# Delta-rule attention in units of 64 tokens of all batches, with the inverse turned on VectorE

## The chip, the core and the metric

The kernel runs on one core of one Trainium2 chip. Its time is the device time of one execution in microseconds (us). A core has TensorE (PE in the profile, its weight loads PEld), VectorE (DVE), ScalarE (ACT), GpSimd (POOL) and SyncE (SP), which here issues every DMA. Each engine works through its own instructions in order and waits for others by semaphores.

## What is computed

```python
k_n = k / (np.linalg.norm(k, axis=-1, keepdims=True) + 1e-06)
state = np.zeros((B, H, D, D), dtype=np.float32)
for t in range(S):
    kt, vt, bt = (k_n[:, :, t], v[:, :, t], beta[:, :, t, None])
    y[:, :, t] = np.einsum('bhd,bhde->bhe', q[:, :, t], state)
    v_old = np.einsum('bhde,bhd->bhe', state, kt)
    state = state + bt[:, :, :, None] * np.einsum('bhd,bhe->bhde', kt, vt - v_old)
...
h = np.maximum(x @ w_in, 0.0)
return (h * h @ w_out).astype(np.float32)
```

B = 4 batches, H = 8 heads, S = 768 tokens, D = 48. `x` is `y` with the heads of a token side by side: 3072 tokens of 384, then an MLP with 2048 hidden units. All in float32.

## The kernel before

**Attention in chunks.** The recurrence is done in chunks of C = 64 tokens. Inside a chunk the tokens depend on each other through a unit lower triangular 64x64 matrix, whose inverse is called T. T is put together from 32x32 blocks (HB = 32): the diagonal blocks are inverted step by step on DVE (`invert`, L383 and L384, 31 steps), and the block below the diagonal comes from two rounds of small matmuls (`whole`, L422 and L430). A unit is 128 tokens (NC = 2 chunks) of two batches; there are 12 units. Partitions 0 to 63 hold one batch of the pair, 64 to 127 the other.

**The steps of a unit.** `load`, `load_q`, `load_v`, `load_beta` fetch rows by DMA. `normalize` (L241 to L254) divides the keys by their norms on ACT and DVE. `static` turns keys and queries by 128x128 transposes on PE (L285), multiplies them (L295), masks (L304), and sends the key products through DRAM (`blocks`, L312, L320) so that each partition of `lt` holds one 32x32 block. `invert` inverts, multiplies by beta (L386), and sends the result through DRAM again (`inv`, L390, L399, L404) into `tt` and `t1t`, which DVE turns (L415). `whole` makes the block below, and multiplies T with the keys (L442) and the values (L449). `sequential` goes through the two chunks: state products (L472), the new state (L485, L488), the output `y` (L493).

**MoE.** `moe` takes the 256 tokens of a unit: it splits `x` into a high and a low half of full speed type (fp32r), so that each product is three matmuls; L541 is the first layer, L528 the second, L548 to L551 and L520 stand between on ACT and DVE.

**The weights.** The 28 weight parts (512 or 384 columns, numbered 0 to 27 here) are split the same way, in the opening of the kernel: `least` is an ACT abs (L142) and a POOL maximum (L143), `words` four DVE operations (L150 to L157) and an ACT copy (L160), `low` three matmuls (L166) and an ACT copy (L167). `far` says how many parts `least` runs ahead: 3 below part AHEAD - 3, 1 from there on. AHEAD is 20.

**What sets the order.** PE, DVE, ACT and SP run in the order in which the program issues (`manual_schedule`); POOL's order is set by the scheduler. `weave` mixes the parts of a unit's attention, at given fractions of the unit, into MoE of the unit before as the filler. In unit 1 the remaining weight splits are mixed in too.

Of the kernel before, what the change touches and what calls it, by code (L numbers as in the profile page):

```python
# [20 lines left out]
def kernel(  # L21
# [14 lines left out]

# [37 lines left out]

    plus, minus = [const.tile([P, P], F32R, name=n) for n in ("plus", "minus")]
# [18 lines left out]
    nc.gpsimd.memset(qp[:, :, :, D:], 0.0)

    ttile = []
    for i in range(2):
        tt = const.tile([P, NC, H, C], F32, name=f"tt{i}")
        nc.gpsimd.memset(tt[:, :, :, :HB], 0.0)
        ttile.append(tt)  # L100
    state = []
    for i in range(NU):
        s = const.tile([P, 2, NP, D], F32, name=f"state{i}")
        nc.gpsimd.memset(s, 0.0)
        state.append(s)

# [13 lines left out]
    AHEAD = 20  # L120
# [67 lines left out]
    def split_bank():  # L188

        turn[1] += 1  # L190
        return (ps_o.tile([P, PC], F32, name=f"o{turn[1] % 2}") if split_early else ps_x.tile([P, PC], F32, name="x"))


    def tokens(x, d):

        t0, b0 = d["t0"], d["b0"]
        return [x[b0 + b, :, t0:t0 + P, :].rearrange("h (c t) d -> t c h d", c=NC) for b in range(2)]

    def load_to(dst, x, d, width):
        for b, src in enumerate(tokens(x, d)):  # L200
            for c in range(NC):
                nc.sync.dma_start(out=dst[b * C:(b + 1) * C, c, :, :width], in_=src[:, c])  # L202

    def load(u):
        t0, b0 = (u // NU) * P, (u % NU) * 2
        d = dict(u=u, t0=t0, b0=b0, y=[None] * NC, marks={})
        d["kp"] = kpad[u % 3]
        load_to(d["kp"], k, d, D)
        return d

    def load_q(d):

        d["qp"] = kpad[2] if d["u"] == 1 else qp
        load_to(d["qp"], q, d, D)

    def load_beta(d):

        first = d["u"] <= 1
        d["bt"] = ds_[0]["bt"] if d["u"] == 1 else apool.tile([P, HB], F32, name="bt", bufs=2)
        t0, b0, x = d["t0"], d["b0"], C * (d["u"] == 1)  # L220

        by = beta[b0:b0 + 2, :, t0:t0 + P].rearrange("b h (c n s) -> b n c h s", n=2, s=HB)
        for n in range(4):
            nc.sync.dma_start(out=d["bt"][x + n * H2:x + (n + 1) * H2], in_=by[n // 2, n % 2])
        if not first:
            nc.sync.dma_start(out=d["bt"][C:], in_=d["bt"][:C])

    def load_v(d):
        d["vt"] = apool.tile([P, NC, H, D], F32, name="vt", bufs=2)
        load_to(d["vt"], v, d, D)  # L230

    def normalize(d):

        n2, s0, s1 = [apool.tile([P, H2], F32, name=f"{n}{d['u'] % 2}", bufs=1) for n in ("n2", "s0", "s1")]
        kn = d["kp"].rearrange("p c h d -> p (c h) d")[:, :, :D]
        for c in range(NC):
            h = slice(c * H, (c + 1) * H)

            sq = (apool.tile([P, H, D], F32, name="r", bufs=2) if d["u"] == 2 else
                  spool.tile([P, PC], F32, name="rest")[:, :H * D].rearrange("p (h e) -> p h e", h=H))  # L240
            nc.scalar.activation(out=sq, in_=kn[:, h], func=AF.Square)  # L241
            nc.vector.tensor_reduce(out=n2[:, h], in_=sq, axis=AX.X, op=ALU.add)  # L242
            yield
# [3 lines left out]
        nc.vector.reciprocal(out=s1, in_=s1)  # L247
        yield
        nc.vector.tensor_tensor(out=s1, in0=s1, in1=n2, op=ALU.mult)
        nc.vector.tensor_tensor(out=s1, in0=s1, in1=s0, op=ALU.add)  # L250
        nc.vector.tensor_scalar(out=s1, in0=s1, scalar1=0.5, scalar2=1e-6, op0=ALU.mult, op1=ALU.add)
        nc.vector.reciprocal(out=s1, in_=s1)
        yield
        nc.vector.tensor_tensor(out=kn, in0=kn, in1=s1.unsqueeze(2).broadcast_to(list(kn.shape)), op=ALU.mult)  # L254
        yield

    def x_tile(u=2):

        turn[0] += 1
        pool, name = (ps_h, "h") if u <= 1 and turn[0] % 4 >= 2 else (ps_x, "x")  # L260
        return pool.tile([P, PC], F32, name=name)


    def static(d):

# [460 lines left out]
```

## Time and profile before

| | us |
|---|---|
| median of 3 runs | 705.74 |
| range of the runs | 704.6 to 705.8 |
| span of the profiled execution | 699.1 |
| PE busy in it | 635.6 (91%) |
| PEld busy | 590.5 (84%) |
| DVE busy | 429.0 (61%) |
| ACT busy | 331.7 (47%) |
| POOL busy | 69.6 (10%) |

The span goes from the first to the last instruction of the profiled execution; the times of the runs hold what lies around it as well, so their median is 6.6 us above the span. The busy shares are means over stages with different limits, and matmuls are pipelined: a busy PE isn't a PE at its peak. The views below are the table of busy times by stretch, the chain of work that ended last (followed back from the last instruction), the timeline, and the groups of like instructions.

### The profile page before, as it was taken

The numbers are of one execution on the slowest core, as the hardware profiler recorded it, in microseconds if no ns is written. First come the engines' busy times: TensorE is split into PE (matmuls) and PEld (weight loads), VectorE is DVE, ScalarE is ACT, GpSimd is POOL, SyncE is SP. The second block draws the span as 40 slices with busy tenths as digits, with TensorE's granted clock in tenths as the row PEclk, the third lists the DMA queues.
The fourth block names the chain that finished last, engine by engine and source line by source line (L and its number), as shares of the span: only waits on it lengthen the run. The fifth ranks groups of instructions, "written<-read, shape, count | busy, mean of one in ns | idle before, by whom it ended". The sixth has DMA issues, their size and how long they took to land.

```text
span 699.1 us, 23322 instructions
## 1 busy us (share of the span) xinstructions
PE 635.6 (91%) x10104; PEld 590.5 (84%) x10104; DVE 429.0 (61%) x1165; ACT 331.7 (47%) x632; POOL 69.6 (10%) x86
## 2 busy tenths in 40 slices
PE   2831789789999999999999999999999999999997
PEld 1610458679999999999999999999999999999996
DVE  4799965677477477486494683775774764731221
ACT  3730665644544544535535535545345355355352
POOL 6540422210101001001001001001010010000000
PEclk9965999999999999999999999999999999999999
DMA  7898504100531522613504405315216124030100
GB/s 160 175 303 312 89 7 80 37 2 12 110 59 24 114 42 38 123 20 54 124 3 80 99 2 112 67 17 116 48 24 123 33 41 91 3 61 3 25 1 23
DMA packets 172134, 49.92 MB, mean 71 GB/s; under 512 B 163840, under 2 KB 166912, under 8 KB 172032
## 3 DMA queue, kind: packets, MB, share of 16 engines
q1 hardware_dynamic: 172032, 48.44, 32.6%
q8 instruction: 79, 1.29, 0.8%
q14 instruction: 23, 0.19, 0.1%
HBM read 37.32 MB, written 11.01 MB: 69 GB/s over the span
## 4 chain that ended last, share of the span: by engine, by line
PE 80%; DVE 9%; SPq 3%; ACT 3%; issue 2%; DMA 1%; POOL 1%; DVEq 0%; POOLq 0%
PE h L541 29%; PE o L528 29%; PE g L472 3%; PE g L493 3%; PE g L449 3%; DVE h_h L381 2%; SPq L202 2%; DVE tt L384 2%; PE x L442 2%; PE x L485 2%; PE x L295 1%; PE g L295 1%; PE g L285 1%; PE x L285 1%; DVE a L153 1%
## 5 line engine op out<-in xcount | busy, mean ns | idle before, releaser
L528 PE MATMUL o<-w,h_h 128*128 128x384 f32 x768 | 203.4, 346 | 0.0
L541 PE MATMUL h<-x_h,w 128*128 128x256 f32 x1152 | 172.3, 285 | 2.2 <-ACT x_h L510 1.3
L520 DVE TENSOR_TENSOR h_l<-r,h_h 128x512 fp32r<-128x512 f32 x96 | 66.4, 691 | 153.0 <-PE o L528 61.7
L541 PEld LDWEIGHTS h<-x_h,w 128*128 128x128 f32 x1152 | 152.6, 188 | 6.1 <-ACT x_h L510 2.7
L548 ACT ACTIVATE r<-h 128x512 f32<-128x512 f32 x96 | 57.4, 598 | 175.1 <-PE h L541 174.8
L528 PEld LDWEIGHTS o<-w,h_h 128*128 128x128 f32 x768 | 133.1, 188 | 2.4
L528 PE MATMUL o<-w,h_l 128*128 128x384 f32 x384 | 129.8, 338 | 0.0
L383 DVE SCALAR_TENSOR_TENSOR tmp<-lt,bt,z 128x126 f32<-128x126 f32 (+22 forms) x310 | 95.8, 309 | 17.6 <-DMA lt<-blocks 8.1
L541 PE MATMUL h<-x_l,w 128*128 128x256 f32 x576 | 99.0, 280 | 0.0
L384 DVE TENSOR_TENSOR z<-z,tmp 128x126 f32<-128x126 f32 (+22 forms) x310 | 79.2, 255 | 10.7
L541 PEld LDWEIGHTS h<-x_l,w 128*128 128x128 f32 x576 | 81.4, 188 | 0.0
L528 PEld LDWEIGHTS o<-w,h_l 128*128 128x128 f32 x384 | 72.1, 188 | 0.0
L549 ACT ACTIVATE r<-r 128x512 f32<-128x512 f32 x96 | 60.7, 632 | 3.1
L551 ACT CAST h_h<-r 128x512 fp32r<-128x512 f32 x96 | 59.5, 620 | 3.1
L367 POOL MEMSET z<- 128x512 f32 x10 | 5.2, 524 | 401.0 <-DMA inv<-z 401.0
L242 DVE TENSOR_REDUCE n<-rest 128x8 f32<-128x384 f32 x22 | 12.0, 550 | 36.7 <-ACT rest L241 36.7
L143 POOL TENSOR_SCALAR a<-a 128x384 f32<-128x384 f32 (+1 forms) x18 | 24.8, 1377 | 55.7 <-ACT a L142 47.1
L166 PE MATMUL o<-r,plus 128*128 128x512 f32 (+1 forms) x16 | 8.8, 637 | 23.0 <-DVE r L153 23.0
L434 ACT ACTIVATE tt<-x 32x256 f32<-32x256 f32 x42 | 15.7, 374 | 26.6 <-PE x L430 26.1
L510 ACT CAST x_h<-h 128x384 fp32r<-128x384 f32 x24 | 11.4, 480 | 31.1 <-PE h L508 31.1
L472 PEld LDWEIGHTS g<-state,kq 48*64 48x64 f32 x1408 | 22.5, 134 | 4.3 <-issue 2.8
L472 PE MATMUL g<-state,kq 48*64 48x48 f32 x1408 | 25.3, 220 | 0.0
(141 smaller groups left out, 783.6 us busy)
## 6 DMA issues: line engine op xcount, KB each, us to landing
w<-in_moe_w_in_dram SPq DMA_DIRECT2D x12, 512.0 KB
w<-in_moe_w_out_dram SPq DMA_DIRECT2D x16, 384.0 KB
lt<-blocks SPq DMA_DIRECT2D x22, 256.0 KB
kpad<-in_k_dram SPq DMA_DIRECT2D x48, 96.0 KB
vt<-in_v_dram SPq DMA_DIRECT2D x48, 96.0 KB
out_dram<-a SPq DMA_DIRECT2D x48, 96.0 KB
qpad<-in_q_dram SPq DMA_DIRECT2D x44, 96.0 KB
blocks<-ap SPq DMA_DIRECT2D x48, 64.0 KB
```

The lines of the kernel that those rows point to most:

```text
L143: nc.gpsimd.tensor_scalar(out=a.bitcast(F32), in0=a.bitcast(F32), scalar1=LEAST, scalar2=None, op0=ALU.max)
L383: nc.vector.scalar_tensor_tensor(out=tmp, scalar=bt[:, s:s + 1], op0=ALU.mult, op1=ALU.mult, **factors)
L384: nc.vector.tensor_tensor(out=z[:, :nj, s + 1:], in0=z[:, :nj, s + 1:], in1=tmp, op=ALU.subtract)
L449: nc.tensor.matmul(g[rows, c, h], lhsT=tt[rows, c, h], rhs=vt[rows, c, h], start=True, stop=True)
L472: nc.tensor.matmul(dst[b * C:(b + 1) * C, j, p], lhsT=kq[rows, c, p, b, x], rhs=s[rows, b, p], start=(x == 0 and p == 0), stop=False, skip ...
L493: nc.tensor.matmul(gy[rows, j, p], lhsT=ap[rows, c, h, 1], rhs=uu[rows, h], start=first and p == 0, stop=True, skip_group_check=True)
L520: nc.vector.tensor_tensor(out=h_l, in0=r, in1=h_h.bitcast(F32), op=ALU.subtract)
L528: nc.tensor.matmul(o[i], lhsT=a[:, e, i * P:(i + 1) * P], rhs=halves["wo", ft][w], start=(ft == 0 and n == 0), stop=(ft == FT - 1 and n == 2))
L541: nc.tensor.matmul(hp[:, e], lhsT=halves["wi", (kt, ft // EACH)][w][:, f], rhs=x[:, kt], start=(n == 0), stop=(n == 3 * KT - 1))
L548: nc.scalar.activation(out=r, in_=hp, func=AF.Relu)
L549: nc.scalar.activation(out=r, in_=r, func=AF.Square)
L551: nc.scalar.copy(out=h_h, in_=r)
```

## The change

A unit is now one chunk of 64 tokens of all four batches (still 12 units). Even and odd heads (j = 0, 1) and batches (b) are laid out so that a head's operands can lie in the other half of the partitions than its result.

- **Raw keys.** Keys aren't normalized. Key products are made of raw keys (`key_products`), 32x32 blocks for two units (a pair) at once; the squared norms are their diagonals, and `prepare` folds the norms into beta and keeps `nr` to scale V (`scale_v`).
- **Turns on DVE.** `load_blocks` loads 32x32 blocks of keys and queries so that one DVE transpose (`turned`) gives the d-by-token form; only the first units use PE (`turned_by_pe`). The trips through DRAM go: DVE turns the key products from PSUM into `lt`, and the inverse into `zt` and `t1` (`ended`).
- **Inverse.** `invert` now always handles full 32-column blocks, for a pair of units at a time: 21 steps in the odd unit (F1 = 21), ten in the next.
- **T inside the chain.** T isn't multiplied with keys and values ahead of time (L442 and L449 go); `state_part` takes V minus the state product, multiplies by T to `w` (L402), then makes state (L412) and output (L418).
- **Splits.** AHEAD is 10. `half_of` draws further splits when MoE needs a half that isn't there.
- PSUM: one pool `g` of two double banks instead of `g` and `x`.

```diff
-    AHEAD = 20
+    AHEAD = 10
...
+    def half_of(key):
+        while key not in halves:
+            next(splits)
+        return halves[key]
...
+    def load_beta(d):
+        d["bt"] = bt = apool.tile([P, HB], F32, name="bt", bufs=1)
...
+        for b in range(2):
+            for s in range(2):
+                for j in range(2):
+                    for i in range(2):
...
+                        nc.sync.dma_start(out=bt[r0:r0 + X],
...
+    def turned(src, dst):
+        nc.vector.transpose(out=dst.rearrange("p n t -> p (n t)"), in_=src.rearrange("p n t -> p (n t)"))
...
+    def key_products(d):
+        d["diag"], low = g_tile(), g_tile()[:, 0]
+        for i in range(2):
+            kt = kts[2 * d["pair"] + i]
+            for x in range(X):
...
+                            half = kt[dims(j), b * X + x, s * HB:(s + 1) * HB]
+                            nc.tensor.matmul(d["diag"][(up, lo)[s](b), j, at], lhsT=half, rhs=half, start=True, stop=True)
...
+                        nc.tensor.matmul(low[(lo, up)[j](b), at], lhsT=first, rhs=second, start=True, stop=True)
...
+        nc.vector.transpose(out=lt.rearrange("p a b -> p (a b)"),
+                            in_=d["diag"].rearrange("p j (c t) -> p t (j c)", t=HB))
...
+    def ended(d):
+        z = d["z"]
+        nc.vector.tensor_tensor(out=z, in0=z, in1=d["bt"].unsqueeze(1).broadcast_to([P, HB, HB]), op=ALU.mult)
...
+        nc.vector.transpose(out=zt.rearrange("p j i x t -> p t (j i x)"), in_=z.rearrange("p s t -> p t s"))
+        yield
+        nc.vector.transpose(out=t1.rearrange("p j i x s -> p s (j i x)"), in_=z.rearrange("p s t -> p (s t)"))
...
-                    nc.tensor.matmul(ps[b][j * C:(j + 1) * C, c, p], lhsT=kp[rows, c, h], rhs=tt[rows, c, h],
-                                     start=True, stop=True)
...
-                    nc.tensor.matmul(g[rows, c, h], lhsT=tt[rows, c, h], rhs=vt[rows, c, h], start=True, stop=True)
...
+                    nc.tensor.matmul(ps[half_rows(b ^ j), j, x], lhsT=tt[half_rows(b), j, x], rhs=vt[half_rows(b), j, x],
+                                     start=True, stop=True)
...
-                    nc.tensor.matmul(gy[rows, j, p], lhsT=ap[rows, c, h, 1], rhs=uu[rows, h],
...
+                    nc.tensor.matmul(gy[half_rows(b), j, x], lhsT=ap[0][half_rows(b ^ j), j, x], rhs=w[half_rows(b ^ j), j, x],
...
+        take(inverse)
+        take(ended(pairs[0]))
         take(splits, 1)
...
+            if u == 1:
+                parts.append((splits, spread(0, 0.88, NW - 6), False))
...
+            if u % 2:
+                parts.append((s, [0.1, 0.5, 0.72], False))
...
+            else:
+                parts.append((inverse, spread(0, 0.26, HB - 1 - F1), True))
+                parts.append((ended(pair), [0.28, 0.30, 0.32], True))
+                parts.append((s, [0.12, 0.56, 0.76], False))
+                parts.append((query_products(u), [0.3], False))
+                parts.append((below(pair, 0), [0.38, 0.45], False))
```

The order moves at three places.

On DVE, in the opening before the first inversion: before, the four operations of a weight part (here part 6) stand ahead of the first inversion (L374 scales `lt` by beta, L381 and L384 are the steps).

```order
L153 SCALAR_TENSOR_TENSOR r<-w_153,r 128x384
L156 TENSOR_SCALAR w_153<-r 128x384
L157 SCALAR_TENSOR_TENSOR h_l<-w_153 128x384
L150 TENSOR_SCALAR a<-a 128x384
L153 SCALAR_TENSOR_TENSOR a<-w_319,a 128x384
L156 TENSOR_SCALAR w_319<-a 128x384
L157 SCALAR_TENSOR_TENSOR rest<-w_319 128x384
L374 TENSOR_TENSOR lt<-lt,bt 128x1024
L381 TENSOR_TENSOR h_h<-lt,tt_110 128x31
```

After the change, on DVE at the same place, the first part (w_130 is part 0) follows the whole inversion and the turns of its result.

```order
L312 TENSOR_TENSOR tmp<-lt,z 128x31
L314 TENSOR_TENSOR z<-z,tmp 128x31
L319 TENSOR_TENSOR z<-z,bt 128x1024
L322 STREAM_TRANSPOSE zt<-z 128x32x32
L324 STREAM_TRANSPOSE t_607<-z 128x32x32
L133 TENSOR_SCALAR a<-a 128x512
L136 SCALAR_TENSOR_TENSOR a<-w_130,a 128x512
L139 TENSOR_SCALAR w_130<-a 128x512
L140 SCALAR_TENSOR_TENSOR rest<-w_130 128x512
```

So parts 0 to 6 have moved from ahead of the first inversion to behind it.

On ACT, among the splits of parts 6 and 7 before: L160 copies the high half of part 6 and of part 7 (w_542, w_708), L167 the low half of the part before, and L142 is the abs of part 9 and of part 10 (w_333, w_335), three ahead.

```order
L160 CAST w_542<-a 128x384
L167 CAST w_505<-o_544 128x384
L142 ACTIVATE r<-w_333 128x512
L241 ACTIVATE r<-kpad_104 128x384 x2
L244 ACTIVATE s_695<-n_694 128x16
L160 CAST w_708<-r 128x512
L167 CAST w_542<-o_710 128x384
L142 ACTIVATE a<-w_335 128x384
```

After, on ACT in unit 1, where L143 copies the high half of parts 11, 12 and 13 (w_1376, w_1398, w_1431), L150 the low half of the part before each, L125 is the abs of parts 12, 13 and 14 (w_494, w_496, w_498), and L288 the square root of the norms.

```order
L143 CAST w_1376<-a 128x384
L150 CAST w_1142<-g 128x384
L125 ACTIVATE a<-w_494 128x384
L143 CAST w_1398<-a 128x384
L150 CAST w_1376<-g 128x384
L125 ACTIVATE a<-w_496 128x384
L288 ACTIVATE s_1415<-lt 128x32
L143 CAST w_1431<-a 128x384
L150 CAST w_1398<-g 128x384
L125 ACTIVATE a<-w_498 128x512
```

The abs now runs one part ahead, from part 7 on instead of from part 17 on, and stands behind the copies of the part before it.

On DVE, in an even unit (unit 2) just ahead of `below`: L246 turns the keys of the unit after next, L319, L322 and L324 are `ended`, L361 masks the query products, L443 is MoE's `h_l`.

```order
L246 STREAM_TRANSPOSE kt<-kb_82 128x1024
L312 TENSOR_TENSOR tmp<-lt,z 128x60
L314 TENSOR_TENSOR z<-z,tmp 128x30x2
L443 TENSOR_TENSOR h_l<-r,h_h 128x512
L312 TENSOR_TENSOR tmp<-lt,z 128x31
L314 TENSOR_TENSOR z<-z,tmp 128x31
L319 TENSOR_TENSOR z<-z,bt 128x1024
L443 TENSOR_TENSOR h_l<-r,h_h 128x512
L361 TENSOR_TENSOR ap<-g,mask 128x512 x2
L322 STREAM_TRANSPOSE zt<-z 128x32x32
L324 STREAM_TRANSPOSE t_2339<-z 128x32x32
L443 TENSOR_TENSOR h_l<-r,h_h 128x512 x2
```

Before, the inversion's steps ran on into the unit and its result left DVE by DMA, with one turn of 256 elements (L415) per unit; now the end of the inversion and the turns stand together in one unit of two.

More of the change, by code (lines that the diff above doesn't have):

```diff
@@ L190, in split_bank @@
         turn[1] += 1
[L191 to L202, printed above, removed]
@@ L228, in load_v @@
[L228 to L243, printed above, removed]
+        return (ps_o.tile([P, PC], F32, name=f"o{turn[1] % 2}") if split_early else g_tile()[:, 0])
@@ L435, in whole @@
         yield
[L436 to L439 removed]
+        if not last:
+            ps = wide(g_tile())
+            for x in range(X):
                 for b in range(2):
[L441 to L443 removed]
@@ L501, in moe @@
-    def moe(d):
+                    for j in range(2):
+                        nc.tensor.matmul(ps[half_rows(j), b, x], lhsT=kp[half_rows(b ^ j), j, x], rhs=w[half_rows(b ^ j), j, x],
+                                         start=True, stop=True)
+            nc.vector.tensor_tensor(out=s, in0=s, in1=ps, op=ALU.add)
+        for x in range(X):
+            for b in range(2):
+                for j in range(2):
+                    nc.tensor.matmul(gy[half_rows(b), j, x], lhsT=ap[0][half_rows(b ^ j), j, x], rhs=w[half_rows(b ^ j), j, x],
+                                     start=first and x == 0, stop=True, skip_group_check=True)
@@ L600, in loads, with weave @@
-    def loads(u):
-        if u + 2 < units:
-            ds_.append(load(u + 2))
-        if u + 1 < units:
-            load_v(ds_[u + 1])
-        yield
-        if u + 2 < units:
-            load_q(ds_[u + 2])
-            load_beta(ds_[u + 2])
-        yield
-        if u + 2 < units:
-            yield from normalize(ds_[u + 2])
-    def state_part(d):
-        yield from whole(d)
-        yield from sequential(d)
-    F0, F1, F2 = 3, 3, 6
-    NS = NW + 1 - (1 + 6 + 4 + 7)
+    def weave(filler, parts):
+        order = [(at, 0, n, gen, quiet) for gen, ats, quiet in parts for n, at in enumerate(ats)]
+        gen, n, a, b = filler
+        order += [(a + (b - a) * (m + 0.5) / n, 1, m, gen, None) for m in range(n)]
+        order = [x[3:] for x in sorted(order, key=lambda x: x[:3])]
+        apart = True
+        while order:
+            gen, quiet = order.pop(0)
+            if quiet is False and not apart and (filler[0], None) in order:
+                order.remove((filler[0], None))
+                next(filler[0], None)
+            next(gen, None)
+            if quiet is not True:
+                apart = quiet is None
@@ L651 @@
         take(splits, 1)
-        for d in pair:
-            take(d, 2)
+        for _ in below(pairs[0], 0):
             take(splits, 1)
-            take(d, 1)
+        for _ in state_part(0):
             take(splits, 1)
-            take(d, 1)
-            take(splits, 1)
-        ds_.append(load(2))
-        fetch(NW)
-        take(invert(ds_[0]))
-        load_v(ds_[1])
-        load_q(ds_[2])
-        load_beta(ds_[2])
-        third = normalize(ds_[2])
-        take(third, 3)
-        for _ in range(3):
-            take(splits, 1)
-            take(third, 1)
```

558 lines of the change are left out of this document (255 added, 303 removed).

## The prediction

> **What bounds the kernel now.** I read the page's head first, then the busy times of stretches, cut at the places where the limit changes.
>
> ```profile
> span 699.1 us, 23322 instructions
> ```
> ```profile
> 0.00:38.60 38.60, 20.81 (x310) 15.37 (x310) 24.87 (x48) 20.12 (x46) 21.05 (x33) 1.00 0.79 170
> 38.60:65.70 27.10, 2.93 (x6) 1.64 (x6) 24.94 (x65) 5.52 (x13) 7.08 (x7) 0.53 1.01 351
> 65.70:104.30 38.60, 29.64 (x514) 18.82 (x514) 31.31 (x64) 23.94 (x51) 13.61 (x11) 0.93 0.31 57
> 104.30:164.90 60.60, 54.00 (x769) 46.93 (x769) 41.66 (x106) 31.98 (x64) 10.28 (x8) 1.00 0.18 35
> 164.90:653.70 488.80, 488.80 (x8238) 468.85 (x8237) 298.53 (x873) 233.00 (x430) 17.59 (x27) 1.00 0.31 59
> 653.70:699.10 45.40, 39.43 (x270) 38.87 (x270) 7.68 (x12) 17.10 (x29) 0.00 (x0) 1.00 0.08 18
> ```
>
> Columns: stretch, length, busy time of PE, PEld, DVE, ACT, POOL, granted clock, DMA share, GB/s. From 164.9 to 653.7 (units 2 to 11) PE is busy without a gap: there a matmul saved is time saved. From 653.7 the last MoE runs alone, and nothing in it changes. Before 164.9 PE isn't the bound: from 38.6 to 65.7 it stands still while DVE inverts T for units 0 and 1, and until 164.9 the splitting of the 28 weight parts sets the pace. So two sums are made, the **opening** and the **ten PE-bound units**.
>
> **The ten units.** The chain that ended last, in one unit (start, us, line, records; each f32 matmul of the program is two records):
>
> ```profile
> 351.42 0.61 PE x L485 x32
> 352.03 0.93 PE g L493 x32
> ...
> 356.35 1.08 PE g L472 x64
> ...
> 364.67 0.33 PE h L508 x3
> ...
> 366.39 0.87 PE x L285 x8
> 367.26 0.87 PE g L285 x8
> 368.14 1.06 PE h L541 x9
> ...
> 372.37 1.03 PE x L295 x32
> 373.40 0.87 PE g L295 x32
> ...
> 381.87 0.68 PE x L422 x50
> ...
> 385.94 0.68 PE x L430 x50
> 386.62 1.25 PE h L541 x9
> ...
> 390.00 1.09 PE x L442 x64
> 391.09 1.85 PE g L449 x64
> ```
>
> L485, L493 and L472 come twice in a unit. Attention thus costs PE 1.22 + 1.86 + 2.16 + 1.74 (L285) + 1.90 (L295) + 0.68 + 0.68 + 1.09 + 1.85 = 13.2 us, 26.4 in two units. MoE's own matmuls stay. L472 and L442, which use all four 64x64 corners of the array, take 1.08 and 1.09 us for 32 matmuls: 34 ns each. L449 and L493, whose operand and result stand in the same half of the partitions (two corners on the diagonal), take 1.85/32 and 0.93/16: 58 ns.
>
> After the change, per unit, L387, L396, L402, L412, L418 and L357 are 32 matmuls each, all with four corners: 6 x 32 x 34 ns = 6.5 us. The transposes L285 and the products L442 go. Per pair of units come 128 matmuls in `below` (32x32, L422's 0.68 us for 32, 21 ns: 2.7 us) and 192 key products L266/L270. These, 48 rows by 32 columns, the trace doesn't show: 21 ns by L422 to 34 ns by L442, 4.1 to 6.5 us; I take 4.1, since the columns match L422's. Two units: 13.0 + 2.7 + 4.1 = 19.8 instead of 26.4, 6.6 less. The first group of MoE behind a piece of attention takes 0.19 longer (L541 x9: 1.25 against 1.06); the pieces fall from 16 to 13 a pair: 0.6 less. Five pairs: 36 us (what the last units lack is 3.6 before and 4.1 after, and cancels). **488.8 becomes 453**, while PE stays the bound.
>
> Does it? DVE's work per unit hardly changes (298.5 of 488.8 before), but it is bunched. These are the rows for it:
>
> ```profile
> 38.64 0.19 DVE L381 TENSOR_TENSOR h_h<-lt,tt 128x31 f32<-128x31 f32 x1
> ...
> 64.20 0.21 DVE L384 TENSOR_TENSOR tt<-tt,h_h 128x31 f32<-128x31 f32 x1
> 64.45 1.23 DVE L386 TENSOR_TENSOR tt<-tt,bt 128x1024 f32<-128x1024 f32 x1
> ```
> ```profile
> L520 DVE TENSOR_TENSOR h_l<-r,h_h 128x512 fp32r<-128x512 f32 x96 | 66.4, 691 | 153.0 <-PE o L528 61.7 <-ACT h_h L551 51.3 <-ACT m L424 36.6
> ...
> L415 DVE STREAM_TRANSPOSE t<-t1t 128x256 f32<-128x256 f32 x12 | 5.3, 438 | 1.0 <-DMA t1t<-inv 1.0
> ```
>
> 31 steps of the full-width inversion take 25.8 us (38.64 to 64.41), so the last ten about 6. A turn of 1024 elements isn't in the trace: between L386's 1.23 and four times L415's 0.438, 1.75; I take 1.28, nearer to L386, since L415's 0.44 for 256 elements holds a fixed part. In an even unit DVE must do, ahead of `below`, ten steps (6), the turn of the keys (1.28), L319 and two turns of T (3.8), five operations of 512 (3.4), three of 384 (1.7, at a little under L520's), and one of 768 (0.96, an estimate between L520's and L386's): 17.2 us, and about 2 more standing behind the state product. PE has 13 MoE groups (13.8), two transposes of y (0.7) and two pieces of attention (2.6) until there: 17.1 us. So PE waits about 2 us at `below`, five times: 10 us (ends: 0, and 4 each if the keys' DMA comes late). **463 us.**
>
> Hidden: the normalizing and V's scaling lie on DVE beside PE; the key DMAs of an even unit have PE's first 9 us as cover, and past it they hold up the turn, priced above. SP issues 52 DMAs in an even unit, at 0.69 us (L224, below) 36 of the unit's 46, so the query turn near the unit's end has its data. The DRAM trips that go were outside PE's path: nothing is gained there in these units.
>
> **The opening.** Weight parts pass ACT (abs), POOL (max), DVE (four operations), ACT (high half), PE, ACT (low half). POOL's starts, and the chain from one to the next:
>
> ```profile
> 94.36 1.16 POOL L143 TENSOR_SCALAR a<-a 128x384 f32<-128x384 f32 x1 [2.82 <-ACT a L142]
> ...
> 121.00 1.49 POOL L143 TENSOR_SCALAR a<-a 128x512 f32<-128x512 f32 x1 [4.12 <-ACT a L142]
> 126.71 1.49 POOL L143 TENSOR_SCALAR a<-a 128x512 f32<-128x512 f32 x1 [4.23 <-ACT a L142]
> 133.98 1.17 POOL L143 TENSOR_SCALAR a<-a 128x384 f32<-128x384 f32 x1 [5.78 <-DVE z L384]
> 138.76 1.16 POOL L143 TENSOR_SCALAR a<-a 128x384 f32<-128x384 f32 x1 [3.62 <-ACT a L142]
> 143.74 1.17 POOL L143 TENSOR_SCALAR a<-a 128x384 f32<-128x384 f32 x1 [3.81 <-ACT a L142]
> 151.77 1.17 POOL L143 TENSOR_SCALAR a<-a 128x384 f32<-128x384 f32 x1 [6.87 <-ACT a L142]
> ```
> ```profile
> 141.72 0.57 DVE rest L157
> ...
> 142.32 0.15 ACT w L160
> ...
> 142.74 0.47 ACT w L167
> 143.21 0.45 ACT a L142
> ```
>
> ACT's next abs stands behind the copies of this part, so with one part ahead the parts run one after another: 4.8 us for 384 columns (133.98 to 138.76), 5.7 for 512 (121.00 to 126.71). Before, 18 parts are through POOL by 94.36 because the look-ahead is three parts up to AHEAD - 3 = 17; ten are left, and unit 2 starts at 164.9. Now it ends at seven, and DVE's order (shown with the change) puts the whole inversion ahead of the first split.
>
> When does the tenth part start? For the beginning:
>
> ```profile
> 6.36 2.77 SPq L224 DMA_DIRECT2D bt<-in_beta_dram  x4
> 9.18 1.35 SPq L128 DMA_DIRECT2D w<-in_moe_w_in_dram  x3
> ```
> ```profile
> 16.23 0.67 ACT L142 ACTIVATE a<-w 128x512 f32<-128x512 f32 x1 [1.02 <-DMA w<-in_moe_w_in_dram]
> ```
>
> Sixteen beta DMAs at 0.69 us stand ahead of the weights on SP: four key loads (about 4 us, an estimate from 0.69 each and their larger size) and 11 us put the weights at about 15 instead of 9.18, the third abs ends at 22.7 (16.9 before), and the square root of the norms waits behind it on ACT. The inversion starts at about 26 instead of 38.64, runs 23 us without POOL beside it (256-element steps, 0.42 + 0.04 each), plus 2.4 of interleaved work and a wait of about 2 for the query products: T at 53.4, turned at 57.2. From there ACT has 28 us of work up to the abs of part 9 (32 copies and conversions of 0.5 to 0.6, `w` and `y` at 0.8, two MoE groups) and waits between for DVE's splits: at the 62% ACT is busy from 65.7 to 104.3 it would be 45 us, without waits 28; my walk through the order gives 39. **Part 9 starts at 96** (85 to 102), where before part 18 starts at 94.36.
>
> From part 9 to part 27 are 18 periods: 9 x 4.8 + 4 x 5.7 + 5 mixed at 5.2 = 92. The nine periods before (five of 4.8, two of 5.7, two mixed) took 57.4 (94.36 to 151.77) where this sum gives 45.8; there the other work of a unit fell between ten parts, now between nineteen, so less of it sticks out: I add 4 (0 to 23) and get 192. The last part's own way (1.2 + 2.0 + 1.5 + 0.9, PE last) 5.6, and five MoE groups behind it 5.6: **unit 2 starts at 203**, 38 later.
>
> Sum: 203 + 463 + 45.4 = 711 us of span, 12 more than 699.1. The runs' median lies 6.6 above this span: **718 us**.
>
> **The rivals.**
>
> *The opening costs less than the units give (faster).* If ACT packs its 28 us without waits (part 9 at 85), the periods stay on their floor (192 becomes 177) and PE never waits at `below`, unit 2 starts at 188: 188 + 453 + 45 + 7 = 693. It turns where unit 2 starts 26 us later than before, at 191, with the waits I take. For it: the periods from 121.00, 133.98 and 138.76 are on the floor; against it: the nine took 11.6 more together. Chance 0.18.
>
> *DVE becomes the bound in even units.* If the turns take 1.75 us and the key DMA (eight issues on SP) holds one up, `below` waits 6 us, not 2: 5 x 4 = 20 more, 738. For: DVE's 17.2 against PE's 17.1; against: odd units leave it slack. Chance 0.14.
>
> *Heads across don't do what is said.* If L402 and L418 stay at L449's 58 ns, 64 x 24 ns in ten units are 15 us: 733. L472 and L442 speak against it. Chance 0.06. [...]
>
> **How the numbers follow.** Forecast 0.62, rivals 0.18, 0.14 and 0.06. The forecast's own range is 708 to 730: part 9's start and the periods' excess carry it. With the key products' 34 ns (10 us) and half of the faster rival inside, 8 in 10 lie from 700 to 738. This kernel's measurement tells 0.2% (1.4 us) from no change. Faster takes its rival's 0.18 and a little of the forecast's edge: 0.19; same 0.04; slower 0.77.
>
> **What would show it.** Right: POOL's last eighteen starts about 5.3 us apart and the first about 26 to 30 us after the turned T; PE without gaps after unit 2 except ahead of `below` in even units; L402 and L418 at 1.1 us for 64 records; two units 93 to 94 us long instead of 98.7. Wrong: unit 2 before 190, or other waits on PE in the steady units, above all behind the turns' DMAs.

## The result, and the profile after

The changed kernel takes 791.84 us (median; runs from 787.46 to 797.49) where the kernel before took 705.17 beside it: 1.125 times as long, 95% interval 1.119 to 1.131. The profiled execution took 788.97, its span is 787.3 (699.1 before). Of all executions below one stands apart and is left out of its kernel's ratio: 1344.91 us, in c5_all, cause unknown.

For reading the traces I cut at the transposes of `y` with which a unit's MoE begins (L508 before, L431 after), first those of unit 2, then those of the tail. Start, us and record, before and after:

```profile
167.06 0.49 PE L508 MATMUL h<-plus,y 128*128 128x128 f32 x3
657.96 0.82 PE L508 MATMUL h<-plus,y 128*128 128x128 f32 x6
```
```profile
223.90 0.49 PE L431 MATMUL h<-plus,y 128*128 128x128 f32 x3
746.53 0.82 PE L431 MATMUL h<-plus,y 128*128 128x128 f32 x6
```

So unit 2 begins 56.8 us later, the ten units between the cuts (the "middle" from here on) take 522.6 us instead of 490.9, and the tail 40.8 instead of 41.1. The forecast had unit 2 begin 38 us later and the middle 26 us shorter. The busy times of these stretches after the change (PE, PEld, DVE, ACT, POOL, then the granted clock, DMA share and GB/s), and of the middle before:

```profile
223.90:746.53 522.63, 477.14 (x9065) 457.25 (x9064) 254.58 (x508) 219.78 (x369) 8.87 (x8) 0.93 0.22 37
746.53:787.30 40.77, 34.95 (x247) 34.41 (x245) 7.67 (x12) 16.33 (x28) 0.00 (x0) 1.00 0.09 20
```
```profile
167.06:657.96 490.90, 490.90 (x8249) 470.95 (x8248) 296.49 (x865) 233.32 (x431) 17.59 (x27) 1.00 0.30 58
```

Two things are new in the middle: PE is idle for 45.5 us (522.63 less 477.14), and its clock, granted in full before, is 0.93 on average. Summing PE's busy time times (1 - granted clock) over stretches of 1 us gives 29.4 us of loss by the clock. What is left, 447.7 us, is PE's work at full clock; before it was 490.9. So the work shrank by 43, and 75 us of something else came in. All of PE's waits in the middle, with what ended them, the sum, the number and the longest:

```profile
PE h L464 <- DVE x_l L434: 11.7, 5, 2.5
PE g L266 <- issue: 9.6, 5, 2.4
PE g L332 <- DVE zt L322: 9.2, 5, 1.8
PE g L333 <- DVE t L324: 7.6, 5, 1.5
PE g L270 <- issue: 5.1, 2, 2.6
PE h L464 <- issue: 2.1, 1, 2.1
```

Three places: the **key products** (9.6 + 5.1 = 14.7 us of "issue", no engine named, in four pairs; the 2.1 at L464 is one more such hole, right behind the last key product of a pair), the MoE's first matmuls, which wait for **`x_l`** (11.7), and **`below`**, which waits for the two turns of T (16.8). Of the clock, one example, stretches of 3 us around `below` in unit 6:

```profile
453.00:456.00 3.00, 3.00 (x58) 2.93 (x51) 2.18 (x3) 0.39 (x1) 0.00 (x0) 1.00 0.03 7
456.00:459.00 3.00, 1.16 (x11) 0.89 (x9) 3.00 (x4) 1.85 (x3) 0.00 (x0) 1.00 0.03 3
459.00:462.00 3.00, 1.49 (x65) 1.37 (x64) 1.51 (x1) 0.31 (x2) 1.36 (x2) 0.61 0.27 61
462.00:465.00 3.00, 3.00 (x11) 3.00 (x11) 0.00 (x0) 2.42 (x5) 0.86 (x1) 0.50 0.68 124
465.00:468.00 3.00, 3.00 (x78) 2.52 (x77) 0.69 (x1) 1.18 (x2) 0.00 (x0) 0.76 0.69 86
```

PE is idle for half of two stretches, and then works for some 6 us at half the clock (it reads 0.50 from 459.6 to 466.6): 11 matmul records in 3 us at 0.50. There are twelve such dips in the middle, all to 0.50, four of them 3.6 us long, seven 7.0 and one 10.6 (by stretches of 0.2 us). They are worth 1.5 to 3.9 us each, 2.4 on average: four behind the key products, five behind `below` and three behind an `x_l` wait.

In the opening, GpSimd's starts (L126, one per weight part) show the pace of the splits:

```profile
84.61 1.49 POOL L126 TENSOR_SCALAR a<-a 128x512 f32<-128x512 f32 x1 [2.38 <-ACT a L125]
102.11 1.48 POOL L126 TENSOR_SCALAR r<-r 128x512 f32<-128x512 f32 x1 [16.02 <-ACT r L125]
107.78 1.16 POOL L126 TENSOR_SCALAR a<-a 128x384 f32<-128x384 f32 x1 [4.19 <-ACT a L125]
112.55 1.17 POOL L126 TENSOR_SCALAR a<-a 128x384 f32<-128x384 f32 x1 [3.60 <-ACT a L125]
126.64 1.17 POOL L126 TENSOR_SCALAR a<-a 128x384 f32<-128x384 f32 x1 [12.92 <-PE o L451]
...
203.90 1.16 POOL L126 TENSOR_SCALAR a<-a 128x384 f32<-128x384 f32 x1 [3.58 <-ACT a L125]
214.40 1.16 POOL L126 TENSOR_SCALAR a<-a 128x384 f32<-128x384 f32 x1 [9.34 <-ACT a L125]
```

Part 9 starts at 102.11 and part 27 at 214.40: 18 periods in 112.3 us. The floor of 4.75 to 5.7 is kept between most; two holes, to 126.64 (9.3 us above the floor) and to 214.40 (5.8), hold 15 us.

### The profile page after: what moved, and what is told of

Its sections match the earlier page's. It is cut to its first block, busy times and chain, and to the rows that moved or that the text cites. A ratio compares the mean times of both kernels' runs of the same rounds, so it can differ in the third digit from the quotient of the medians.

```text
span 787.3 us, 25119 instructions
## 1 busy us (share of the span) xinstructions
PE 644.2 (82%) x11368; PEld 592.5 (75%) x11368; DVE 381.9 (49%) x777; ACT 313.0 (40%) x544; POOL 53.8 (7%) x55
## 4 chain that ended last, share of the span: by engine, by line
PE 65%; DVE 18%; issue 6%; ACT 3%; SPq 2%; DMA 2%; POOL 1%; DVEq 0%; POOLq 0%
PE h L464 25%; PE o L451 23%; DVE tmp L312 3%; DVE z L314 3%; PE g L149 2%; PE g L266 2%; PE g L387 2%; PE g L357 2%; PE g L402 1%; DVE zt L322 1%; PE g L412 1%; PE g L418 1%; DVE h_l L443 1%; DVE rest L140 1%; PE g L396 1%
## 5 line engine op out<-in xcount | busy, mean ns | idle before, releaser
L464 PE MATMUL h<-x_h,w 128*128 128x256 f32 x1152 | 186.4, 300 | 24.3 <-DVE x_l L434 12.6
L443 DVE TENSOR_TENSOR h_l<-r,h_h 128x512 fp32r<-128x512 f32 x96 | 66.0, 688 | 258.1 <-PE o L451 163.2
L464 PEld LDWEIGHTS h<-x_h,w 128*128 128x128 f32 x1152 | 166.6, 204 | 29.7 <-issue 15.4
L464 PE MATMUL h<-x_l,w 128*128 128x256 f32 x576 | 105.8, 295 | 0.3
L464 PEld LDWEIGHTS h<-x_l,w 128*128 128x128 f32 x576 | 88.1, 203 | 0.9 <-DVE x_l L434 0.9
L314 DVE TENSOR_TENSOR z<-z,tmp 128x31 f32<-128x31 f32 (+15 forms) x186 | 64.0, 344 | 6.4
L312 DVE TENSOR_TENSOR tmp<-lt,z 128x31 f32<-128x31 f32 (+15 forms) x186 | 62.6, 337 | 4.2 <-DVE lt L302 0.5
L143 ACT CAST w<-a 128x384 fp32r<-128x384 f32 (+1 forms) x23 | 12.7, 553 | 86.8 <-DVE rest L140 86.8
L149 PE MATMUL g<-a,plus 128*128 128x384 f32 (+1 forms) x42 | 24.6, 674 | 21.5 <-ACT w L150 16.2
L266 PE MATMUL g<-kt 48*32 48x32 f32 x1536 | 25.8, 225 | 15.3 <-issue 15.3
L126 POOL TENSOR_SCALAR a<-a 128x384 f32<-128x384 f32 (+1 forms) x23 | 29.7, 1292 | 112.9 <-ACT a L125 89.0
L266 PEld LDWEIGHTS g<-kt 48*32 48x32 f32 x1536 | 23.5, 124 | 17.2 <-issue 16.6
L332 PE MATMUL g<-zt,mt 32*32 32x32 f32 x384 | 11.9, 211 | 27.5 <-DVE zt L322 27.5
L270 PE MATMUL g<-kt 48*32 48x32 f32 x768 | 24.8, 223 | 10.1 <-issue 9.2
L332 PEld LDWEIGHTS g<-zt,mt 32*32 32x32 f32 x384 | 9.8, 122 | 29.7 <-issue 18.8
```

Of the source, the lines that this page charges most:

```text
L126: nc.gpsimd.tensor_scalar(out=a.bitcast(F32), in0=a.bitcast(F32), scalar1=LEAST, scalar2=None, op0=ALU.max)
L149: nc.tensor.matmul(ps, lhsT=m, rhs=y, start=(n == 0), stop=(n == 2))
L266: nc.tensor.matmul(d["diag"][(up, lo)[s](b), j, at], lhsT=half, rhs=half, start=True, stop=True)
L270: nc.tensor.matmul(low[(lo, up)[j](b), at], lhsT=first, rhs=second, start=True, stop=True)
L312: nc.vector.tensor_tensor(out=tmp, op=ALU.mult, in0=lt[:, s:s + 1, s + 1:].broadcast_to([P, nj, nt]), in1=z[:, :nj, s:s + 1].broadcast_to( ...
L314: nc.vector.tensor_tensor(out=z[:, :nj, s + 1:], in0=z[:, :nj, s + 1:], in1=tmp, op=ALU.subtract)
```

## The experiments

Each kernel is the changed one with the edit shown. The figures for the middle are made as above. "Work" is the middle less idle time and clock loss; the time's ratio is to the kernel before, run beside it (medians from 702.3 to 705.2), with its 95% interval. Executions of one kernel differ by up to 10 us (787 to 797 for the changed one), and the middle's figures come from a single one, for some (e2_below_later, c3_steady) the fastest: a difference of a few us between two middles is not shown by them.

| kernel | median us | ratio | unit 2's cut | middle | idle | clock loss | work |
|---|---|---|---|---|---|---|---|
| before | 705.17 | 1 | 167.1 | 490.9 | 0.0 | 0.0 | 490.9 |
| changed | 791.84 | 1.125 (1.119-1.131) | 223.9 | 522.6 | 45.5 | 29.4 | 447.7 |
| e1_kp_spread | 778.24 | 1.105 (1.101-1.109) | 227.4 | 508.1 | 34.2 | 19.2 | 454.7 |
| e2_below_later | 775.52 | 1.102 (1.098-1.106) | 221.0 | 508.1 | 38.2 | 18.6 | 451.3 |
| e3_early | 788.18 | 1.120 (1.116-1.124) | 227.0 | 520.0 | 44.0 | 26.7 | 449.3 |
| e5_filled | 787.78 | 1.119 (1.115-1.122) | 225.8 | 519.7 | 30.9 | 23.1 | 465.7 |
| e4_opening | 765.32 | 1.089 (1.085-1.093) | 199.0 | 522.8 | 46.0 | 28.5 | 448.3 |
| e6_sooner | 787.72 | 1.120 (1.115-1.124) | 219.6 | 522.8 | 45.3 | 29.0 | 448.5 |
| e7_ahead | 760.54 | 1.083 (1.077-1.088) | 194.3 | 523.6 | 47.5 | 27.2 | 448.9 |
| c3_steady | 756.08 | 1.076 (1.070-1.082) | 222.2 | 487.8 | 22.7 | 9.8 | 455.3 |
| c4_all | 729.95 | 1.039 (1.034-1.044) | 200.5 | 486.6 | 22.3 | 8.3 | 456.0 |
| c6_all | 720.98 | 1.027 (1.022-1.032) | 189.7 | 491.7 | 23.9 | 13.0 | 454.8 |
| c5_all | 703.52 | 1.002 (0.999-1.005) | 190.5 | 469.2 | 11.1 | 1.6 | 456.5 |
| c7_all | 700.66 | 0.998 (0.996-1.000) | 189.4 | 470.4 | 11.3 | 2.8 | 456.3 |
| c8_all | 690.38 | 0.984 (0.982-0.987) | 183.5 | 463.8 | 7.0 | 0.0 | 456.8 |

### The key products in pieces

```diff
                         nc.tensor.matmul(low[(lo, up)[j](b), at], lhsT=first, rhs=second, start=True, stop=True)
+                if d["pair"] > 1 and x % 4 == 3 and (i, x) != (1, X - 1):
+                    yield
...
+    KP0, KP1, NKP = 0.11, 0.235, X // 2
...
-                    parts.append((key_products(nxt), [0.18], False))
+                    parts.append((key_products(nxt), [0.18] if u == 1 else spread(KP0, KP1, NKP), False))
```

> The 384 small key products of a pair are no longer issued in one piece but in eight pieces of 48 between MoE matmuls (pairs 2 to 5; pair 1 as in the changed kernel). Theory: in one piece they run faster than TensorE's instructions arrive (idle 'issue' of 3.7 us per pair, 14.7 us in the middle, no engine named), and such a hole brings the granted clock down for about 6 us, worth some 2.4 us a time (29.4 us for 12 dips). Then four holes and four dips go: 4 x (3.7 + 2.4) = 24 us less than the changed kernel's 791.8, so about 767. Rival: the hole is a price per small matmul, whatever stands between them: the idle time spreads and the time stays at 792. Second rival: the clock is low for another reason than holes (more matmuls in four corners at once): holes go, dips stay, 777.

(The 384 are records, two for each of 192 matmuls.) The pieces are four of 96 records, not eight of 48: X is 8, so the new line yields after x = 3 and x = 7 of both units, and NKP is 4. In one pair of this kernel they begin at 392.65 and here:

```profile
394.87 0.29 PE L266 MATMUL g<-kt 48*32 48x32 f32 x15
397.23 0.29 PE L266 MATMUL g<-kt 48*32 48x32 f32 x15
399.45 0.29 PE L266 MATMUL g<-kt 48*32 48x32 f32 x15
```

It gained 14 us, not 24. Idle time fell by 11.3 and the clock loss by 10.2, as the theory has it, and all four dips behind the key products went; so neither rival holds. The work rose by 7.0, which I had left out. That would be 0.6 us for each of the 12 added pieces, but the cause isn't shown: in e2_below_later, which adds no piece, it rose by 3.6. What such a hole looks like can be seen in the changed kernel. In the pair near 395 us, the first matmuls behind each hole, one stretch of 0.4 us in the first hole and one just behind it, and the DMA queues in the two stretches of 0.4 us just ahead of the holes (395.2 and 399.2; packets, MB, share):

```profile
398.25 0.21 PE L270 MATMUL g<-kt 48*32 48x32 f32 x1 [2.65 <-issue]
401.71 0.28 PE L266 MATMUL g<-kt 48*32 48x32 f32 x6 [1.84 <-issue]
```
```profile
395.60:396.00 0.40, 0.01 (x1) 0.00 (x0) 0.00 (x0) 0.00 (x0) 0.00 (x0) 1.00 0.13 31
398.40:398.80 0.40, 0.40 (x52) 0.40 (x52) 0.00 (x0) 0.00 (x0) 0.00 (x0) 0.50 0.86 196
```
```profile
q8 instruction: 1, 0.02, 21.0%
...
q8 instruction: 1, 0.02, 15.0%
```

One packet of the instruction queue moves just ahead of each of the two holes. Over the whole middle that queue shows:

```profile
q8 instruction: 71, 1.16, 0.9%
```

71 packets for 9,065 matmul and 9,064 weight-load records: 255 of these records a packet, and a packet every 7.4 us on average (522.6 / 71). By that ratio, an estimate that counts TensorE's records alone, the 768 records of the key products are three packets in about 4 us of work. Broken up, with MoE matmuls between, they lose 5.5 us to "issue" where it was 14.7. That instructions arrive late, as the theory has it, stays a guess: whether the packet itself is late, or something behind it, no row shows.

### The products below the diagonal, later

```diff
-                parts.append((below(pair, 0), [0.38, 0.45], False))
+                parts.append((below(pair, 0), [0.46, 0.52], False))
```

> The products below the diagonal of the even unit stand 0.08 and 0.07 of a unit (about 4 us) later among the MoE steps. Theory: their wait for the two turns on VectorE (1.8 + 1.5 us in each of five even units, 16.8 us) goes and with it five clock dips of about 2.4 us: 29 us less, about 763. Rival: VectorE's queue is full there, and the wait moves to the next reader (x_l, or T in the product with the values): less than 10 us gained, about 785.

16 us gained. The wait at L332 is gone, the one at L333 is not (the PE waits of this kernel's middle):

```profile
PE g L333 <- DVE t L324: 7.6, 5, 1.5
```

PE comes to `below` only about 2 us later, measured from the query products, since the steps in the list are whole MoE groups; the two kinds of product stand alternately, so the second turn still holds both. Three of the five dips behind `below` are gone all the same.

### The inversion sooner

```diff
-                    parts.append((key_products(nxt), [0.18], False))
-                    parts.append((prepare(nxt), spread(0.24, 0.32, 6), True))
-                    parts.append((inverse, spread(0.34, 1, F1), True))
+                    parts.append((key_products(nxt), [0.18 if u == 1 else 0.03], False))
+                    parts.append((prepare(nxt), spread(0.24, 0.32, 6) if u == 1 else spread(0.1, 0.18, 6), True))
+                    parts.append((inverse, spread(0.34, 1, F1) if u == 1 else spread(0.2, 1, EARLY), True))
```

> Key products, norms and inversion of the next pair start 0.15 of a unit (8 us) earlier in the odd unit, in one piece as before (pairs 2 to 5). Theory: VectorE runs behind by some 4 us from the inversion's start on, so its 8 us of new room end both the wait for x_l (11.7 us in the middle) and that for the turns (16.8), with five to eight dips of 2.4: 40 to 47 us less, about 748; the issue holes at the key products (14.7) and their four dips stay. Rival: VectorE is full for the whole pair, so the lag returns: 785 to 792.

(EARLY is 25.) The theory fell: nothing to speak of was gained, and `below` waits as long as before. A late start of VectorE isn't what makes `below` wait. The changed kernel's VectorE ahead of `below` in unit 6 shows why (the query products L357 run on PE from 452.41):

```profile
452.89 1.22 DVE L319 TENSOR_TENSOR z<-z,bt 128x1024 f32<-128x1024 f32 x1
454.93 0.69 DVE L443 TENSOR_TENSOR h_l<-r,h_h 128x512 fp32r<-128x512 f32 x1 [0.82 <-PE o L451]
455.54 1.28 DVE L361 TENSOR_TENSOR ap<-g,mask 128x512 f32<-128x512 f32 x2
456.74 2.02 DVE L322 STREAM_TRANSPOSE zt<-z 128x1024 f32<-128x1024 f32 x1
458.62 1.89 DVE L324 STREAM_TRANSPOSE t<-z 128x1024 f32<-128x1024 f32 x1
```

The turns stand behind `h_l`, which waits for PE, and behind the mask of the query products, which PE makes just then. From 454.93 to 460.51 VectorE works without a pause, and PE is at `below` at 456.97 (458.81 less its wait of 1.84). However early the inversion ends, the turns come 8 us behind the start of the query products (8.1 here, 8.1 in e3_early). `x_l` is held up by the list too, though not by a wait for PE: ahead of it, behind the last `h_l`, stand five steps of the inversion (two operations each) and V's scaling, and PE is idle from 440.66 to 443.11.

```profile
436.89 0.69 DVE L443 TENSOR_TENSOR h_l<-r,h_h 128x512 fp32r<-128x512 f32 x1
...
439.15 0.95 DVE L372 TENSOR_TENSOR vt<-vt,nr 128x768 f32<-128x768 f32 x1
...
442.13 0.37 DVE L314 TENSOR_TENSOR z<-z,tmp 128x207 f32<-128x207 f32 x1
442.42 0.55 DVE L434 TENSOR_TENSOR x_l<-h,x_h 128x384 fp32r<-128x384 f32 x1
```

### The wait filled with matmuls

```diff
-        ps = g_tile()[:, 0, :X * HB].rearrange("p (x t) -> p x t", x=X)
+        g = g_tile()
+        ps = g[:, 0, :X * HB].rearrange("p (x t) -> p x t", x=X)
+        for n in range(20 if i == 0 and d["pair"] else 0):
+            nc.tensor.matmul(g[:, 1, :DM], lhsT=plus, rhs=half_of(("wo", n % 8))[0], start=True, stop=True)
         for x in range(X):
             for b in range(2):
                 nc.tensor.matmul(ps[up(b), x], lhsT=mt[lo(b), i, x], rhs=zt[lo(b), 0, i, x], start=True, stop=True)
```

> Ahead of the first products below the diagonal of each even unit stand 20 matmuls of 128x384 whose result nobody reads (about 3.6 us at full clock), where TensorE idles 3.3 us now. If idle time is what lowers the granted clock, the five dips behind this place go, and the fillers only take the place of the wait: 5 x 2.4 = 12 us less, about 780. If the clock is lowered by something else, the dips stay at their places and the time is 792 to 796.

The same place, unit 6, in this kernel (the fillers run from 458.03 for 3.64 us, `below` starts at 461.60):

```profile
458.00:461.00 3.00, 3.00 (x20) 3.00 (x19) 3.00 (x3) 1.86 (x3) 0.00 (x0) 1.00 0.03 3
461.00:464.00 3.00, 2.68 (x75) 2.27 (x74) 1.11 (x1) 1.04 (x3) 1.76 (x2) 1.00 0.47 103
464.00:467.00 3.00, 3.00 (x81) 2.71 (x81) 0.69 (x1) 2.74 (x5) 0.46 (x1) 1.00 0.35 66
```

The clock stays at 1.00 where it was 0.50, in all five units: so at this place PE's idle time was what lowered it. The time hardly moved, though: five fillers of 3.6 us (18 us of work more) took the place of 15 us of idle time, and the dips behind the key products, which weren't touched, lasted 11 us each here against 7 to 11, and all five `x_l` waits had one, so that the clock loss fell by 6.3 and not by 12.

### The opening: a third pair of work tiles, two parts sooner, twelve parts ahead

```diff
+        if x >= AHEAD and x % 3 == 2:
+            return [spool.tile([P, PC], I32, name=y, bufs=1)[:, :n] for y in ("a2", "rest2")]
...
-            far = 3 if x < AHEAD - 3 else 1
+            far = 3 if x < AHEAD - 3 else 2
...
```

> Parts 10 to 27 of the weights get a third pair of work tiles and are begun two ahead instead of one. Theory: the 18 periods of the opening (112.3 us from part 9 to part 27 on GpSimd, 6.2 each) are a chain over ScalarE, GpSimd, VectorE, TensorE with one part in flight; with two in flight a period falls to about 4.5, so unit 2 begins about 28 us sooner (196 instead of 224) and the time is about 763. Rival: TensorE's own work at a clock of 0.80 between 80 and 224 us (97.9 us busy) and the holes at the key products bound the opening: less than 8 us gained, 784 or more.

```diff
         take(key_products(pairs[0]))
-        take(splits, 1)
+        take(splits, 3)
         take(prepare(pairs[0]))
```

> Two parts of the weights are split ahead of the first norms, while VectorE idles (its first 22 us). Theory: each part that leaves the queue behind T saves a period of 4.5 to 5.7 us later on, less what the norms are delayed: 4 to 10 us less than 791.8, about 785. Rival: the weights arrive no sooner than the keys, the norms wait by as much as is saved: 792.

```diff
-    AHEAD = 10
+    AHEAD = 20
...
         for _ in below(pairs[0], 0):
-            take(splits, 1)
+            take(splits, 4)
         for _ in state_part(0):
-            take(splits, 1)
+            take(splits, 4)
```

> The changed kernel with 17 instead of 9 parts of the weights split ahead of unit 1 (four in each place ahead of it instead of one, three parts in flight for them), as the kernel before did. Theory: ahead of the MoE a part takes about 3.2 us, behind it 6.2; eight parts moved save some 24 us, and unit 2 begins at about 196 to 200 instead of 224: time about 766. Rival: the first unit's attention waits behind the eight parts by as much (25 us), and nothing is gained: 790.

All three came near their theories: unit 2's cut at 199.0, 219.6 and 194.3, times 765, 788 and 761. The 4 us of e6_sooner lie within the spread of the runs. e7_ahead was near its theory by luck: in the program's order VectorE splits 17 parts ahead of unit 1 where the changed kernel splits 5, so twelve moved, not eight, and at the theory's price (6.2 less 3.2 us) that is 36 us, where 29.6 came. Two parts in flight, or the parts split ahead of unit 1, are each worth 25 to 30 us: the opening was set by the chain of one part at a time behind unit 0, not by PE. The middle didn't change in any of them.

### Both causes together

`c3_steady` puts the key products in two pieces (it yields after the eight `x` of the pair's first unit; its theory below says four) at the start of the odd unit, and moves the steps of the steady units:

```diff
+                if d["pair"] > 1 and x % 8 == 7 and (i, x) != (1, X - 1):
+                    yield
...
+    KP0, KP1, NKP = 0.0, 0.08, 2 * X // 8
...
+                    parts.append((key_products(nxt), [0.18] if u == 1 else spread(KP0, KP1, NKP), False))
+                    parts.append((prepare(nxt), spread(0.24, 0.32, 6) if u == 1 else spread(0.1, 0.18, 6), True))
+                    parts.append((inverse, spread(0.34, 1, F1) if u == 1 else spread(0.2, 0.84, 22), True))
...
+                parts.append((inverse, spread(0, 0.26, HB - 1 - F1) if u == 2 else spread(0.1, 0.22, 9), True))
+                parts.append((ended(pair), [0.28, 0.30, 0.32] if u == 2 else [0.24, 0.26, 0.28], True))
...
+                parts.append((below(pair, 0), [0.44, 0.51], False))
```

> For the units from 3 on: key products at the start of the odd unit in four pieces, norms and inversion behind them, and no inversion step between 0.84 of the odd unit and 0.1 of the even one, so that x_l isn't behind a row of steps; turns 0.04 of a unit earlier and the products below the diagonal 0.06 later. Theory: the middle's idle time (45.5 us) falls below 12 and its clock loss (29.4) below 8, TensorE's own work rises from 448 to about 452 with the added switches: middle 472 instead of 522.6, time about 741. Rival: VectorE, tied to TensorE by the h_l tiles, stays late wherever the steps stand, and half of the idle time remains: 765.

756: halfway. The `x_l` waits are gone but for one (1.9 us), so these steps were in its way. 7.4 us of "issue" and 9.9 at `below` stayed. `c4_all` is this with e4_opening's edit.

> The two edits together (third pair of work tiles in the opening, and the steady units' new order). If both causes are apart, the gains add: about 713; at best the time before, 704. If the opening is bound by TensorE, about 735.

730: the gains add, and the middle is c3_steady's. `c5_all` has four pieces (its theory below says eight), spread over 0.12 of the unit, `below` at 0.48 and 0.54, the state product of the odd unit at 0.2 instead of 0.1, and the edits of e4_opening, e6_sooner and e7_ahead; `c6_all` is c4_all, so with two pieces, with e6_sooner's edit and three parts instead of one at each place ahead of unit 1.

> All edits together: key products in eight pieces at the odd unit's start, the steady units' new order with the products below the diagonal 0.04 later again, 17 parts ahead of unit 1, two in flight behind, two parts ahead of the norms. If the gains add: unit 2 at 185 or sooner, the middle 475, 41 + 6.6 behind: 707; if the eight parts ahead only delay unit 1, about 725.

> As c5_all with key products in four pieces at the start, products below the diagonal as in c3_steady, and 13 parts ahead of unit 1. If the gains add: unit 2 at 192, middle 484, 41 + 6.6 behind: 724. Against c5_all it shows whether the holes of four pieces (7.4 us in the middle of c3_steady) go with eight.

c5_all took 703.5 (no difference to before can be told), c6_all 721. With four pieces and the later `below` the middle loses 11.1 us of idle time and 1.6 by the clock, against 23.9 and 13.0 in c6_all; no wait at the key products is put down to "issue" any more (7.5 in c6_all). The pieces begin 3.4 to 4.6 us apart here, 2.2 to 3.3 (their holes included) in e1_kp_spread, which also had four and lost 5.5. From unit 3 to unit 9 two units take 93.6 to 94.3 us by their cuts, as forecast. The middle:

```profile
190.45:659.69 469.24, 458.16 (x9065) 437.99 (x9064) 261.22 (x511) 219.13 (x369) 8.87 (x8) 1.00 0.25 41
```

Unit 2 still begins at 190. In c5_all one stretch of unit 1 has VectorE doing nothing at all, and ahead of the next split stands `h_l`, waiting for PE, which is at the key products of pair 1 in one piece from 134.3 to 142.3 and, behind them, at MoE with its clock down:

```profile
140.00:150.00 10.00, 8.17 (x74) 6.26 (x74) 0.00 (x0) 3.90 (x7) 1.16 (x1) 0.74 0.01 2
```
```profile
150.31 0.69 DVE L447 TENSOR_TENSOR h_l<-r,h_h 128x512 fp32r<-128x512 f32 x1 [13.81 <-PE o L455]
```

`c7_all` fetches three weight parts ahead of beta and splits one more ahead of the norms. `c8_all` also takes the key products and norms of pair 1, and `below` of unit 1, ahead of unit 1, and gives units 1 and 2 the steady order:

```diff
+        for _ in below(pairs[0], 1):
+            take(splits, 1)
         for _ in state_part(0):
             take(splits, 1)
...
+        for n, _ in enumerate(key_products(pairs[1])):
+            take(splits, (0, 1)[n % 2])
+        for n, _ in enumerate(prepare(pairs[1])):
+            take(splits, (0, 1)[n % 2])
```

> c5_all with the first three weight parts fetched ahead of beta, and three parts instead of two split ahead of the first norms. In c5_all VectorE idles to 25.3 us and is over nine tenths busy from 40 to 110. If VectorE sets the opening, work that moves into its idle start shortens it: 4 to 8 us less than c5_all's 703.5, about 698. If the weights land no sooner, or the norms wait for the added part (2.6 us), 702 to 706.

> c7_all with the key products, norms and second corner of pair 1 (and unit 1's products below the diagonal) ahead of unit 1, in pieces between the splits, and with the steady order for units 1 and 2 too. In c5_all VectorE does nothing from 140 to 150 us: it waits for TensorE behind the key products of pair 1, and the splits wait with it (12 us on GpSimd). If that wait and its clock dip are what is left of the opening, unit 2 begins some 12 us sooner (175 to 180): about 688. If VectorE's own work ahead of unit 1 (now some 5 us more) takes it back, 698 to 703.

c7_all gained 3 us, and unit 2 began 1 us sooner. The weights landed little sooner (VectorE's first operation on them starts at 23.95 instead of 25.34), so VectorE's idle start was hardly filled, and whether its work sets the opening stays open. c8_all took 690.4, less than either kernel (0.984 of the time before, 0.982 to 0.987). Its opening is 5.9 us shorter than c7_all's, half of what was expected, and its middle 6.6 us shorter, which I hadn't counted; that the sum came to the expected 688 is luck:

```profile
183.54:647.31 463.77, 456.71 (x9066) 437.05 (x9064) 257.65 (x500) 219.24 (x369) 8.89 (x8) 1.00 0.25 42
```

7 us of idle time, and the clock at 1.00 throughout. Unit 2 still begins 16 us later than in the kernel before; what sets that wasn't separated.

## Why the prediction was wrong

It said slower, by 12 us; it was 87. The direction was right through the opening alone; the middle went the other way, and no rival came near. By its own terms, with unit 2's start 2.2 us ahead of the cut:

- **PE's work, 453 (455 between these cuts): right.** Measured 447.7 at full clock. Heads across cost what was said: 64 records of L402 or L418 take 1.11 and 1.12 us, as forecast 1.1. So that rival is out.

```profile
L418 PE MATMUL g<-w,ap 64*64 64x48 f32 x640 | 11.2, 218 | 0.0
L402 PE MATMUL g<-vt,tt 64*64 64x48 f32 x640 | 11.1, 218 | 0.0
```

- **"PE waits about 2 us at `below`", 10 us in all: too small, and by the wrong sum.** It was 3.4 us a time, 16.8 in all. I had set VectorE's whole work from the unit's start against PE's (17.2 and 2 against 17.1). What ends the wait is a short piece of order: `h_l` and the mask, which follow PE, and behind them two turns. The turns were under-sized too, 3.8 for both and L319 together with 1.2 for that; they alone took 2.02 and 1.89. Both write with a stride of 32 elements, and L322 reads with one too; L246, contiguous on both sides, takes 1.25 (forecast 1.28), and L284, which reads PSUM with that stride and writes contiguously, no more:

```profile
131.25 1.24 DVE L284 STREAM_TRANSPOSE lt<-g 128x1024 f32<-128x1024 f32 x1
```

e3_early, which gave VectorE 8 us more room and left the wait as it was, showed that VectorE's total isn't what counts, and thereby that the rival "DVE becomes the bound" had the right place and the wrong mechanism.
- **"PE stays the bound", with no other wait: this is the step that failed.** Of three kinds of stall the forecast priced one. 11.7 us at `x_l` came from the same bunching, at a place I hadn't walked through; 14.7 at the key products, whose 21 ns I had priced as work but not as a run of 768 instructions.
- **The clock: missing altogether.** I took the granted clock of 1.00 in the steady units as given; behind waits of PE of 1.2 to 2.65 us it fell to 0.50. 29.4 us of the middle are lost there, more than at any of the waits. Idle time of 35.5 us above the forecast's 10, the clock's 29.4, and 7 less work make the middle 522.6 instead of 465 (the forecast's 463 between these cuts). c8_all is the check: with 7.0 us of idle time, no wait above 0.6 us and the clock at 1.00 the middle takes 463.8.
- **The opening, 203: 18.7 too short** (221.7). T was turned at 62.6 instead of 57.2: the inversion began at 29.4, not 26, and the turns cost more. From there to part 9 it took 39.5 us, forecast 38.8. (Under "What would show it" I had written 26 to 30 us for this, which contradicts that sum.) The 18 periods took 112.3 instead of 96, inside the range's 115. In both holes the splits stand behind an `h_l` that waits for PE: in the first PE is at the key products of pair 1 with their holes and half a clock, in the second at the state products and MoE.

```profile
128.72 0.69 DVE L443 TENSOR_TENSOR h_l<-r,h_h 128x512 fp32r<-128x512 f32 x1 [12.96 <-PE o L451]
```

Behind the last period 4 us were saved. So here a size was off, "I add 4", not the mechanism; e4_opening and e7_ahead confirmed the one-ahead chain as its cause.

## What to carry to other kernels

A saving on an engine that runs without a gap holds only if the new order leaves no gap: every new wait costs itself and can cost half clock behind it (here 1.5 to 3.9 us behind waits of 1.2 to 2.65 us, one or two close together; not always: two of the five `x_l` waits didn't), so count the waits one by one at the instruction that stands ahead of each on its queue, not by the sums of busy time. Break long runs of tiny matmuls up with large ones between them, and put an operation that TensorE waits for ahead of those that themselves follow TensorE, as c5_all does with the turns and the mask (not tested alone). The change itself was sound: with its order mended and the opening's edits, it is 1.6% faster than the kernel it replaced. That gain lies in the middle, since unit 2 still begins later; whether the opening's edits would speed up the kernel before as well wasn't tested.

## What the hardware showed

- Around a run of 384 small matmul records (768 with their weight loads, in about 4 us of work) TensorE stood still twice, for 1.2 to 2.65 us each, with no engine named that it waited for (in one of the four pairs the second time came right behind the run). In four pieces between MoE matmuls, begun 2.2 to 3.3 us apart, the runs lost 5.5 us in the middle of e1_kp_spread; in four pieces 3.4 to 4.6 us apart, as in c5_all, every wait at them had a named engine.
- Behind idle stretches as short as these the granted clock halved: at 398.4, 2.8 us after PE stopped, it was 0.50, and it stayed there until 405. The `x_l` wait of 2.45 us brought it down in three of four units; the fourth time, and behind the one `x_l` wait of 1.86 us, it stayed at 1.00. What makes this difference no run here shows. The dips took 29.4 of the middle's 522.6 us.
- A turn of 128x1024 on VectorE takes 1.24 to 1.25 us where it writes contiguously (L246, and L284, which reads PSUM with a stride of 32 elements), and 1.86 to 2.02 where it writes with that stride (L322 and L324, six times each in the changed kernel).
